# Moving batch 1's value chunks and key burst, and one unit pair of batch 2, in a block-sorted attention and SwiGLU kernel

## The chip, the cores and the metric

The kernel runs on one core of a Trainium2 chip. The core has a matrix engine (TensorE, PE in the profile, with its weight loads as PEld), three engines for the rest (VectorE or DVE, ScalarE or ACT, GpSimd or POOL), a queue engine for DMAs (SyncE or SP), and 16 DMA engines. The metric is the device time of one execution in microseconds (us). The kernel before takes 247.38 us, the median of three runs (247.33 to 247.43).

## The reference

Four batches, eight heads, 768 positions, head width 64. Keys and values are cut into eight blocks of 96 positions and mixed with a small matrix that five rounds of row and column normalisation make nearly doubly stochastic; then each block of queries attends to its mixed block. The result, 3072 tokens of width 512, goes through a SwiGLU feed-forward layer of inner width 1536.

```python
for _ in range(5):
    P = np.exp(P - np.max(P, axis=-1, keepdims=True))
    P = P / (np.sum(P, axis=-1, keepdims=True) + 1e-09)
    P = P / (np.sum(P, axis=-2, keepdims=True) + 1e-09)
k_sorted = np.einsum('bhij,bhjcd->bhicd', P, k_b)
v_sorted = np.einsum('bhij,bhjcd->bhicd', P, v_b)
attn = softmax(scale * q_b @ k_sb^T)            # block by block, 96 x 96
x = (attn @ v_sb), heads side by side           # 3072 x 512
g = x @ w_gate
out = (g * sigmoid(g) * (x @ w_val)) @ w_out    # 3072 x 512
```

## The kernel before

The tokens are worked on in eight half batches of 384 tokens. Half batch `n` (batch `n // 2`, half `n % 2`) has one **pass** of the feed-forward layer, `ffn(n)`: 12 gate bursts and 12 value bursts of four matmuls each (L410, L428), and, for the half batch before, three output tiles in three parts of four matmuls each (L445). The attention of a later half batch is worked in between these. A pass is written as `merge(ffn(n), side)` (L599): `ffn(n)` is a list of pieces with a cost (0.65 for a gate or value burst, 0.87 for an output part), `side` a list of pieces with a due time, and a side piece is issued after the first main piece with which the summed cost reaches its due time. `merge` sets the order on TensorE and GpSimd, which follow the program; in these passes the order on VectorE, ScalarE and SP is made by the scheduler when the kernel is built.

The side pieces:

- `kqs(b, ats)` (L588): three **key bursts** (with the queries) for a batch; each is two chunks of 32 matmuls (L269), the first into tile "b" and drained by VectorE, the second into tile "a" and drained by ScalarE.
- `vs(v_chunk, 16, ats)` (L592): batch 1's four **value chunks**, 16 matmuls each (L300), into "b", "a", "b", "a". In the string `"sssv"` s is ScalarE and v is VectorE: the engine that drains the chunk into `vt`.
- `units(b, us, ats, avs)` (L572): eight units per batch, in pairs. At `at` the **scores** of both units (`qk`, L332; the first into "b", the second into "a") with the first exp; at `at + 1.3` the second exp (L345, ScalarE); at `at + avs[0]` and `at + avs[1]` the attention times values (`av`, L359, into "b" and "a"), each followed by a reciprocal `r_sb` (L363) and a product `st` (L365) on VectorE and, from batch 1 on, by a transposing DMA on SP (L391) that writes a quarter of `xt`, the input of that half batch's pass.

"a" and "b" are one PSUM tile each: whoever writes one waits until its last reader is done. The gate, value and (in the second pass) output tiles rotate through three buffers called "gen", so each waits for the reader of the tile three before it. Outputs from the third pass on use a tile of their own, "x".

Behind a gate burst ScalarE computes `th` (tanh, L418) and VectorE `gs` (L420); behind a value burst VectorE computes `h` (L433). An output tile is copied by ScalarE (L450) and written by SP (L452). POOL issues `q_cast` (L394), which writes the queries of batches 2 and 3 to a scratch in DRAM, early in the second pass, and then waits at `hold` (L639) for the last quarter of batch 1's first `xt` before it loads the values of batches 2 and 3.

The passes of this case are the second, `ffn(1)` (L636), which holds batch 1's keys, values and first four units, the third, `ffn(2)` (L645), which reads the `xt` made there, and the fourth, `ffn(3)` (L647), with batch 2's first four units.

Of the kernel before, what the change touches and what calls it, by code (L numbers as in the profile page):

```python
# [17 lines left out]
def kernel(  # L18
# [226 lines left out]
    def drain(eng, dst, src):  # L245
        if eng == "v":
            nc.vector.tensor_copy(dst, src)  # L247
        else:
            nc.scalar.copy(dst, src)  # L249
# [13 lines left out]
    def kq_chunk(b, at, n, eng, tag):  # L263
        dst = kqt_tile(b)[:, 0:2 * GI * C].rearrange("p (n c) -> p n c", c=C)
        rm = rmix[b].rearrange("p a (g two) i -> p two (a g) i", two=2)
        tp = chunk_tile("tkq", n // 8, tag).rearrange("p (l n) -> p l n", n=2 * GI)
        for lc in range(n):
            for two in range(2):
                nc.tensor.matmul(tp[two * D:(two + 1) * D, lc, :],  # L269
                                 lhsT=kq_at(b, at + lc),  # L270
                                 rhs=rm[:, two], start=True, stop=True)
        drain(eng, dst[:, :, at:at + n], tp.transpose([0, 2, 1]))
# [31 lines left out]
    def v_pair_chunk(pair, at, n, eng, tag):  # L304
        dst = vt_tile(pair)[:, :, :, at:at + n]
        tp = chunk_tile("tv", n // 4, tag).rearrange("p (u l n) -> p u l n", u=2, n=H * NB)
        for ld in range(n):
            col = (at + ld) * C
            for u, rows in enumerate((lowr, highr)):
                nc.tensor.matmul(tp[:, u, ld, :], lhsT=vch[rows, col:col + 128],  # L310
                                 rhs=rmix["p"][rows, u].rearrange("p a b -> p (a b)"),
                                 start=True, stop=True)
        drain(eng, dst, tp[0:C].transpose([0, 1, 3, 2]))
# [4 lines left out]
    def scores(b, u, tag):  # L318
        half, g = divmod(u, H2)
        k_sb, k_at, q_sb, q_at = ((kqts[b], 0, kqts[b], GI * C) if b < 2 else  # L320
                                  (kqts["p"], (b - 2) * GI * C, kqts["q"], (b - 2) * GI * C))
        if tag == "gen":
            wide = None
            pss = [bank_tile("qk"), bank_tile("qk")]
        else:
            wide = pair_tile("qk", tag).rearrange("p (two n) -> p two n", two=2)
            pss = [wide[:, 0], wide[:, 1]]
        for i4 in range(4):
            at = (g * NB + half * 4 + i4) * C
            for two in range(2):  # L330
                lo = two * D
                nc.tensor.matmul(pss[two][:, i4 * C:(i4 + 1) * C],  # L332
                                 lhsT=k_sb[lo:lo + D, k_at + at:k_at + at + 128],
                                 rhs=q_sb[lo:lo + D, q_at + at:q_at + at + C],
                                 start=True, stop=True)
        return wide, pss

    def exps(b, u, wide, pss):
        n = ecount[0] % 8
        ecount[0] += 2  # L340
        if wide is None:
            for two in range(2):
                nc.scalar.activation(e_all[:, n + two, 0:4 * C], pss[two][0:C, 0:4 * C], AF.Exp, scale=scale)
        else:
            nc.scalar.activation(e_all[:, n:n + 2, 0:4 * C], wide[0:C, :, 0:4 * C], AF.Exp, scale=scale)  # L345
        es[(b, u)] = [e_all[:, n, :], e_all[:, n + 1, :]]

    def qk(b, u, tag="b"):
        exps(b, u, *scores(b, u, tag))

    def av(b, u, tag="a"):
        half, g = divmod(u, H2)
        vt = vts[b // 2][:, b % 2].rearrange("p (h i) e -> p h i e", h=H)
        av_ps = pair_tile("av_ps", tag).rearrange("p (two n) -> p two n", two=2)
        o = av_ps.rearrange("p two (i e) -> p two i e", i=4)
        for two in range(2):
            e = es[(b, u)][two]
            for i4 in range(4):
                nc.tensor.matmul(o[:, two, i4, 0:D + 1], lhsT=e[:, i4 * C:i4 * C + 128],  # L359
                                 rhs=vt[:, 2 * g + two, half * 4 + i4, 0:D + 1],  # L360
                                 start=True, stop=True)
        r_sb = ssp.tile([C, 2, 4, 1], FP32, name="r_sb", tag="r")
        nc.vector.reciprocal(r_sb, o[0:C, :, :, D:D + 1])  # L363
        st = ssp.tile([C, 4, 2, D], BF16, name="st", tag="st")
        nc.vector.tensor_tensor(st.rearrange("p i two d -> p two i d"), o[0:C, :, :, 0:D],  # L365
                                r_sb.to_broadcast([C, 2, 4, D]), op=ALU.mult)
        sts[(b, u)] = st
# [11 lines left out]
    def xtr(b, u):  # L379
        half, g = divmod(u, H2)  # L380
        if g == 0:
            xts[(b, half)] = xtp.tile([128, H2, TW], BF16, name=f"xt{b}_{half}", tag="xt")
        x_ps = xt_tile("x", 1)[:, 0]
        x_to(x_ps, b, u)
        return xts[(b, half)][:, g, :], x_ps.rearrange("p a b -> p (a b)")

    def x_dma(b, u):
        half, g = divmod(u, H2)
        if g == 0:
            xts[(b, half)] = xtp.tile([128, H2, TW], BF16, name=f"xt{b}_{half}", tag="xt")  # L390
        nc.sync.dma_start_transpose(out=xts[(b, half)][:, g, :].rearrange("p (i c) -> p i c", c=C),  # L391
                                    in_=sts.pop((b, u)).rearrange("p i two d -> p (i two d)"))
# [179 lines left out]
    def units(b, us, ats, avs=(1.9, 3.6), lag=3.1):  # L572
        us = list(us)
        todo = []
        for n, at in enumerate(ats):
            u, u2 = us[2 * n:2 * n + 2]
            held = []
            todo.append((at, lambda u=u, u2=u2, held=held: (qk(b, u, "b"), held.append(scores(b, u2, "a")))))
            todo.append((at + 1.3, lambda u2=u2, held=held: exps(b, u2, *held[0])))
            for w, tag, t in ((u, "b", avs[0]), (u2, "a", avs[1])):  # L580
                if b == 0:
                    todo.append((at + t, lambda w=w, tag=tag: av(b, w, tag)))
                    todo.append((at + t + lag, lambda w=w: drain("v", *xtr(b, w))))
                else:
                    todo.append((at + t, lambda w=w, tag=tag: (av(b, w, tag), x_dma(b, w))))
        return todo

    def kqs(b, ats):  # L588
        return [(at, lambda n=n: (kq_chunk(b, n * 32, 16, "v", "b"), kq_chunk(b, n * 32 + 16, 16, "s", "a")))
                for n, at in enumerate(ats)]  # L590

    def vs(f, size, ats):  # L592
        return [(at, lambda m=m: f(1, m * size, size, "sssv"[m], "ba"[m % 2])) for m, at in enumerate(ats)]

    def v_pairs(ats):
        return [(at, lambda m=m: (v_pair_chunk(1, m * 16, 8, "v", "b"), v_pair_chunk(1, m * 16 + 8, 8, "s", "a")))
                for m, at in ats]

    def merge(main, side):  # L599
        done, k = 0.0, 0  # L600
        side = sorted(side, key=lambda t: t[0])
        for c, f in main:
            f()
            done += c
            while k < len(side) and side[k][0] <= done:
                side[k][1]()
                k += 1
        while k < len(side):
            side[k][1]()
            k += 1  # L610

    def ffn(n):
        todo = []
        for m in range(NFC):
            if n > 0 or m > 1:
                todo.append((0.65, lambda m=m: gate(n, m)))
            if n > 0 or m > 0:
                todo.append((0.65, lambda m=m: value(n, m)))
            ends = (7, 9, 11) if n == 1 else (3, 7, 11)
            if n > 0 and m in ends:  # L620
                for part in range(3):
                    todo.append((0.87, lambda t3=ends.index(m), part=part: outp(n - 1, t3, part)))
        return todo
# [7 lines left out]
    def q0_rest():  # L631
        q0_chunk(1, 0, 16, "s", "b")
        q0_chunk(1, 16, 8, "v", "a")

    merge(ffn(0), [(0.0, q0_rest)] + units(0, range(4, 8), (2.0, 6.6)))
    merge(ffn(1), kqs(1, (0.6, 3.3, 7.8)) + vs(v_chunk, 16, (5.2, 6.5, 9.1, 10.4))  # L636
          + units(1, range(4), (11.0, 15.6), (1.3, 2.6)))
    hold = const.tile([1, 1], BF16)
    nc.gpsimd.tensor_copy(hold, xts[(1, 0)][0:1, H2 - 1, 0:1])  # L639
# [2 lines left out]
    for s in range(4):  # L642
# [1 line left out]
    nc.vector.memset(kqt_tile("p")[:, 2 * GI * C:], 0.0)  # L644
    merge(ffn(2), units(1, range(4, 8), (0.0, 5.5)) + kqs("p", (13.0, 14.7, 20.7)) + v_pairs([(0, 22.5)])  # L645
          + [(13.0, lambda: q_dma(2)), (16.4, lambda: q_dma(3))])
    merge(ffn(3), v_pairs([(1, 0.0), (2, 5.1), (3, 6.9)]) + units(2, range(4), (9.8, 14.0)))  # L647
    merge(ffn(4), units(2, range(4, 8), (0.0, 8.0)))
    merge(ffn(5), units(3, range(4), (0.0, 8.0)))
    merge(ffn(6), units(3, range(4, 8), (0.0, 8.0)))  # L650
# [36 lines left out]
```

## Time and profile before

| what | us |
| --- | --- |
| median of the runs | 247.38 |
| profiled execution | 247.53 |
| its span, first to last instruction | 245.7 |
| gate matmuls, L410 (376 in the records) | 76.6 |
| value matmuls, L428 (380) | 77.3 |
| output matmuls, L445 (276) | 64.4 |
| `th` on ScalarE, L418 (96) | 47.1 |
| `gs` on VectorE, L420 (96) | 52.9 |
| `h` on VectorE, L433 (96) | 53.3 |
| exps on ScalarE, L345 (30) | 22.6 |
| casts of `vt` on ScalarE, L249 (10) | 9.1 |
| casts of `vt` on VectorE, L247 (8) | 8.6 |
| third pass's first gate starts at | 75.72 |
| fifth pass's first gate starts at | 134.25 |

Of a few hundred matmuls some records are missing (384 gate matmuls are issued, 376 are recorded). In a timeline row the columns are start, length, engine, line, operation, output and input, count, and in brackets the idle time before it with what ended it. Matmuls are pipelined: the length of a burst of four is given as 0.81 us, while such bursts follow one another every 0.65 us. A burst's price is therefore read from starts, not from lengths.

### The profile page before, as it was taken

The numbers are of one execution on the slowest core, as the hardware profiler recorded it, in microseconds if no ns is written. First come the engines' busy times: TensorE is split into PE (matmuls) and PEld (weight loads), VectorE is DVE, ScalarE is ACT, GpSimd is POOL, SyncE is SP. The second block draws the span as 40 slices with busy tenths as digits, with TensorE's granted clock in tenths as the row PEclk, the third lists the DMA queues.
The fourth block names the chain that finished last, engine by engine and source line by source line (L and its number), as shares of the span: only waits on it lengthen the run. The fifth ranks groups of instructions, "written<-read, shape, count | busy, mean of one in ns | idle before, by whom it ended". The sixth has DMA issues, their size and how long they took to land.

```text
span 245.7 us, 6163 instructions
## 1 busy us (share of the span) xinstructions
PE 237.1 (97%) x2617; PEld 139.4 (57%) x2617; DVE 155.9 (63%) x327; ACT 111.2 (45%) x188; POOL 51.3 (21%) x45
## 2 busy tenths in 40 slices
PE   7799999998999999999999999999999999999994
PEld 5375666675555565555555655565555555555543
DVE  6786789877564685777655845664675576445700
ACT  3977653465444535365542543265235424332311
POOL 5992139990002059300000000000000000000000
PEclk9999999999999999999999999999999999999999
DMA  5989999999995999510121211112111211110122
GB/s 95 216 121 209 206 213 211 206 213 190 156 131 143 196 136 157 139 43 3 45 75 32 61 59 37 41 53 69 32 43 45 75 36 43 43 43 3 43 85 85
DMA packets 39642, 24.77 MB, mean 101 GB/s; under 512 B 29376, under 2 KB 34368, under 8 KB 39616
## 3 DMA queue, kind: packets, MB, share of 16 engines
q0 software_dynamic: 19632, 14.16, 38.7%
q1 hardware_dynamic: 19840, 10.17, 17.4%
q8 instruction: 20, 0.33, 0.6%
q10 hardware_dynamic: 144, 0.07, 0.1%
q14 instruction: 6, 0.05, 0.1%
HBM read 28.32 MB, written 7.86 MB: 147 GB/s over the span
## 4 chain that ended last, share of the span: by engine, by line
PE 86%; DVE 6%; issue 2%; DMA 2%; ACT 2%; DVEq 0%; POOLq 0%
PE v_ps L428 24%; PE g_ps L410 24%; PE o_ps L445 24%; PE tkq L269 3%; PE av_ps L359 3%; PE qk L332 3%; DMA v<-in_v_dram 2%; DVE st L365 1%; DVE vt L247 1%; DVE gs_sb L420 1%; PE o_ps L461 1%; PE idle_ps L477 1%; DVE h L433 1%; PE tq L279 1%; PE tv L300 1%
## 5 line engine op out<-in xcount | busy, mean ns | idle before, releaser
L420 DVE SCALAR_TENSOR_TENSOR gs_sb<-th_sb,g_ps 128x384 bf16<-128x384 bf16 x96 | 52.9, 551 | 49.5 <-ACT th_sb L418 46.4
L428 PE MATMUL v_ps<-xt,wv_sb 128*128 128x384 bf16 x380 | 77.3, 326 | 0.1
L410 PE MATMUL g_ps<-xt,wg_sb 128*128 128x384 bf16 x376 | 76.6, 325 | 0.2
L418 ACT ACTIVATE th_sb<-g_ps 128x384 bf16<-128x384 f32 x96 | 47.1, 491 | 56.2 <-PE g_ps L410 53.6
L445 PE MATMUL o_ps<-wo,h 128*128 128x512 bf16 x276 | 64.4, 379 | 0.0
L433 DVE SCALAR_TENSOR_TENSOR h<-v_ps,gs_sb 128x384 bf16<-128x384 f32 x96 | 53.3, 556 | 7.6 <-DVE gs_sb L420 0.5
L428 PEld LDWEIGHTS <-wv_sb 128*128 128x128 bf16 x380 | 35.5, 97 | 24.0 <-issue 0.7
L410 PEld LDWEIGHTS <-wg_sb 128*128 128x128 bf16 x376 | 34.8, 97 | 23.7 <-issue 0.6
L445 PEld LDWEIGHTS <-h 128*128 128x128 bf16 x276 | 26.0, 98 | 28.4
L450 ACT COPY o_sb<-o_ps 128x512 f32<-128x512 f32 x23 | 13.5, 586 | 46.0 <-PE o_ps L445 46.0
L148 POOL COPY vch<-v 64x1536 bf16<-64x1536 bf16 (+2 forms) x11 | 28.8, 2658 | 13.3 <-DMA v<-in_v_dram 13.3
L345 ACT ACTIVATE e_all<-qk 96x768 bf16<-96x768 f32 x30 | 22.6, 802 | 8.1 <-PE qk L332 8.1
L365 DVE TENSOR_TENSOR st<-av_ps,r_sb 96x512 bf16<-96x512 f32 x32 | 21.8, 680 | 0.3
L359 PEld LDWEIGHTS <-e_all 96*128 96x128 bf16 x256 | 11.9, 97 | 5.2 <-ACT e_all L345 0.9
L363 DVE RECIPROCAL r_sb<-av_ps 96x8 f32<-96x8 f32 x32 | 6.4, 199 | 11.5 <-PE av_ps L359 11.5
L359 PE MATMUL av_ps<-vt,e_all 96*128 96x65 bf16 x256 | 13.1, 193 | 0.0
L249 ACT CAST vt<-tv 96x1024 bf16<-96x1024 f32 (+1 forms) x10 | 9.1, 923 | 5.6 <-PE tv L310 3.6
L247 DVE CAST vt<-tv 96x1024 bf16<-96x1024 f32 (+1 forms) x8 | 8.6, 1082 | 2.2 <-PE tv L310 1.7
L477 PE MATMUL idle_ps<-warm_sb 128*128 128x512 bf16 x25 | 6.9, 382 | 0.0
L247 DVE COPY oq_v<-o_ps 128x128 f32<-128x128 f32 x1 | 0.3, 293 | 9.3 <-PE o_ps L461 9.3
L395 POOL DMA_DIRECT2D q_scr<-in_q_dram x2 | 5.6, 3178 | 0.0
L146 ACT COPY vch<-v 64x768 bf16<-64x768 bf16 (+1 forms) x4 | 5.5, 1388 | 0.3 <-DMA v<-in_v_dram 0.3
(83 smaller groups left out, 130.2 us busy)
## 6 DMA issues: line engine op xcount, KB each, us to landing
out_dram<-o_sb SPq DMA_DIRECT2D x23, 256.0 KB, 2.0
v<-in_v_dram POOLq DMA_DIRECT2D x4, 384.0 KB, 12.7
wg_sb<-in_moe_w_gate_dram POOLq DMA_DIRECT2D x3, 512.0 KB, 11.4
wv_sb<-in_moe_w_val_dram POOLq DMA_DIRECT2D x3, 512.0 KB, 13.2
wo<-in_moe_w_out_dram POOLq DMA_DIRECT2D x3, 512.0 KB, 16.0
kqp<-in_k_dram POOLq DMA_DIRECT2D x2, 768.0 KB, 10.1
q_scr<-in_q_dram POOLq DMA_DIRECT2D x2, 768.0 KB, 17.8
v<-in_v_dram POOLq DMA_DIRECT2D x2, 768.0 KB, 9.8
```

Source lines behind the costliest of these rows:

```text
L148: eng.tensor_copy(dst, src.transpose([0, 2, 1]))
L247: nc.vector.tensor_copy(dst, src)
L345: nc.scalar.activation(e_all[:, n:n + 2, 0:4 * C], wide[0:C, :, 0:4 * C], AF.Exp, scale=scale)
L359: nc.tensor.matmul(o[:, two, i4, 0:D + 1], lhsT=e[:, i4 * C:i4 * C + 128], rhs=vt[:, 2 * g + two, half * 4 + i4, 0:D + 1], start=True, sto ...
L365: nc.vector.tensor_tensor(st.rearrange("p i two d -> p two i d"), o[0:C, :, :, 0:D], r_sb.to_broadcast([C, 2, 4, D]), op=ALU.mult)
L410: nc.tensor.matmul(g_ps, lhsT=wg_sb[:, kc, ts(m, 128)], rhs=xt[:, kc, :], start=(kc == 0), stop=(kc == NKC - 1))
L418: nc.scalar.activation(th_sb, g_ps, AF.Tanh, scale=0.5)
L420: nc.vector.scalar_tensor_tensor(gs_sb, th_sb, 1.0, g_ps, op0=ALU.add, op1=ALU.mult)
L428: nc.tensor.matmul(v_ps, lhsT=wv_sb[:, kc, ts(m, 128)], rhs=xt[:, kc, :], start=(kc == 0), stop=(kc == NKC - 1))
L433: nc.vector.scalar_tensor_tensor(h_tiles[n][:, m, :], v_ps, 0.5, gs_tiles.pop(m), op0=ALU.mult, op1=ALU.mult)
L445: nc.tensor.matmul(o_ps, lhsT=h_w[:, m, ts(t3, 128)], rhs=wo_sb[part][:, m % 4, :], start=(m == 0), stop=(m == NFC - 1))
L450: nc.scalar.copy(o_sb, o_ps)
```

## The change

Three edits, all in due times and one string:

- In the second pass the last three value chunks are due at 5.8, 8.4 and 9.1 instead of 6.5, 9.1 and 10.4, and the third key burst at 7.1 instead of 7.8. The second value chunk now follows gate burst 4 instead of value burst 4; the third key burst follows gate 5 instead of value 5; the third value chunk follows gate 6 instead of value 6; the fourth follows value 6 instead of value 7.
- The fourth value chunk is drained by ScalarE instead of VectorE.
- In the fourth pass batch 2's second unit pair is due at 14.9 instead of 14.0. Its scores follow the third part of the second output tile instead of its second part, its first `av` follows value burst 8 instead of gate burst 8, and its second `av` follows gate burst 10 instead of value burst 9.

```diff
     def vs(f, size, ats):
-        return [(at, lambda m=m: f(1, m * size, size, "sssv"[m], "ba"[m % 2])) for m, at in enumerate(ats)]
+        return [(at, lambda m=m: f(1, m * size, size, "s", "ba"[m % 2])) for m, at in enumerate(ats)]
...
-    merge(ffn(1), kqs(1, (0.6, 3.3, 7.8)) + vs(v_chunk, 16, (5.2, 6.5, 9.1, 10.4))
+    merge(ffn(1), kqs(1, (0.6, 3.3, 7.1)) + vs(v_chunk, 16, (5.2, 5.8, 8.4, 9.1))
           + units(1, range(4), (11.0, 15.6), (1.3, 2.6)))
...
-    merge(ffn(3), v_pairs([(1, 0.0), (2, 5.1), (3, 6.9)]) + units(2, range(4), (9.8, 14.0)))
+    merge(ffn(3), v_pairs([(1, 0.0), (2, 5.1), (3, 6.9)]) + units(2, range(4), (9.8, 14.9)))
```

With it the scheduler's order moves in three places. On VectorE the drain of the third key burst stands ahead of `h` of value burst 5 instead of behind it, and the cast of the fourth value chunk is gone. On ScalarE the casts of the third and fourth value chunks stand together ahead of `th` of gate burst 7. In the fourth pass the copy of the second output tile stands ahead of the second pair's two exps instead of behind them, and VectorE's `r_sb`, `st`, `gs` and `h` of gate and value bursts 8 to 10 take another order: `gs`, `r_sb`, `h`, `st` of the first unit, then the second unit's `r_sb` and `st` behind `gs` and around `h` of burst 10. SP's and GpSimd's orders are the same.

## The prediction

> **What bounds the kernel now.** First the page. The profiled execution took 247.53 us with a span of 245.7 us at full granted clock; the median of the runs shown is 247.38 us.
>
> ```profile
> span 245.7 us, 6163 instructions
> PE 237.1 (97%) x2617; PEld 139.4 (57%) x2617; DVE 155.9 (63%) x327; ACT 111.2 (45%) x188; POOL 51.3 (21%) x45
> PE 86%; DVE 6%; issue 2%; DMA 2%; ACT 2%; DVEq 0%; POOLq 0%
> ```
>
> TensorE works 97% of the span and is 86% of the chain that ended last. The change keeps every matmul, so it can only win or lose TensorE's idle time in the two passes it touches. One pass is one `merge(ffn(n), ...)`. From start of one pass to the next I read 32.6 us for the second (43.1 to 75.72) and 28.5 us for the fourth (105.78 to 134.25).
>
> Second, the waits of TensorE: the longest single one is a score matmul waiting for a value chunk drained by VectorE. The timeline shows where (start, length, engine, line, operation).
>
> ```profile
> PE qk L332 <- DVE vt L247: 1.0, 1, 1.0
> ...
> 59.02 0.63 PE L300 MATMUL tv<-rmix,vch 128*128 128x64 bf16 x16
> 59.49 1.03 PE L445 MATMUL o_ps<-wo,h 128*128 128x512 bf16 x4
> 60.45 0.34 PE L332 MATMUL qk<-kqt 64*128 64x96 bf16 x8
> 60.49 1.21 DVE L247 CAST vt<-tv 96x1024 bf16<-96x1024 f32 x1
> 61.75 0.35 PE L332 MATMUL qk<-kqt 64*128 64x96 bf16 x8 [0.96 <-DVE vt L247]
> 62.03 1.90 PE L445 MATMUL o_ps<-wo,h 128*128 128x512 bf16 x8
> ```
>
> The fourth value chunk (59.02) fills tile "a"; its VectorE drain starts at 60.49, behind `gs` and `h` of the FFN, and ends at 61.70; the second half of the scores needs "a". Bursts follow each other by start-to-start pitch: gate or value 0.65 us, output part 0.87, `av` 0.245, a pair of scores 0.45 (118.64 to 119.09 below), key burst 1.13, value chunk 0.47, and 0.09 more before scores or a key burst (117.90 to 118.64 is 0.74). So the output part after these scores was due at 60.45 + 0.45 = 60.90 and came at 62.03: 1.13 us lost. Another 0.19 is lost where the third value chunk starts at 57.26 instead of 56.42 + 0.65 = 57.07, waiting for VectorE's drain of the third key burst.
>
> Third, the fourth pass around batch 2's two unit pairs.
>
> ```profile
> 118.64 0.51 PE L332 MATMUL qk<-kqtq,kqtp 64*128 64x96 bf16 x16
> 119.03 1.50 ACT L345 ACTIVATE e_all<-qk 96x768 bf16<-96x768 f32 x2 [0.47 <-PE qk L332]
> 120.43 0.49 ACT L418 ACTIVATE th_sb<-g_ps 128x384 bf16<-128x384 f32 x1
> 120.64 0.81 PE L410 MATMUL g_ps<-xt,wg_sb 128*128 128x384 bf16 x4
> 120.95 0.55 DVE L420 SCALAR_TENSOR_TENSOR gs_sb<-th_sb,g_ps 128x384 bf16<-128x384 bf16 x1 [1.14 <-ACT th_sb L418]
> 121.55 0.81 PE L428 MATMUL v_ps<-xt,wv_sb 128*128 128x384 bf16 x4
> ...
> 124.27 0.77 PE L332 MATMUL qk<-kqtq,kqtp 64*128 64x96 bf16 x16
> 124.97 1.04 PE L445 MATMUL o_ps<-wo,h 128*128 128x512 bf16 x4
> ```
>
> The second pair's scores (124.27 to 124.97) take 0.70 instead of 0.45: 0.25 lost waiting for "a", which VectorE's `st` frees at 124.64. The first pair teaches more: two exps hold ScalarE from 119.03, so the `tanh` of the gate issued just after the scores starts at 120.43, its `gs` ends at 121.50, and the value matmul that reuses that gate's bank (three banks rotate) starts at 121.55 instead of 120.64 + 0.65 = 121.29.
>
> Fourth, the transposing DMAs that bring batch 1's first half to the third pass, on SP's queue.
>
> ```profile
> q0 software_dynamic: 2467, 0.31, 246.2%
> ...
> 70.53 2.16 SPq L391 DMA_TRANSPOSE xt<-st  x1
> 72.74 0.58 SPq L452 DMA_DIRECT2D out_dram<-o_sb  x1
> 73.37 1.22 SPq L391 DMA_TRANSPOSE xt<-st  x1
> ...
> 75.74 0.18 POOL L639 COPY hold<-xt 1x1 bf16<-1x1 bf16 x1 [20.82 <-DMA xt<-st]
> ```
>
> The first line is the DMA view of 64 to 66 us: only the software queue (the `q_cast` writes) moves, though SP issued an output at 64.58 and a transpose at 65.17; these land after the writes, which end near 71. The fourth transpose, at 73.37, has landed when POOL's `hold` starts (75.74); the pass's first gate (75.72) needs it for its fourth matmul at 75.72 + 0.49 = 76.21. Slack about 0.5 us.
>
> **Second pass, worked out.** PE issues the same bursts in the order gate 4, value chunk 2, value 4, gate 5, key burst 3, value 5, gate 6, chunk 3, value 6, chunk 4, gate 7, value 7, output, scores. From gate 4 at 51.47 the pitches give chunk 2 at 52.12, key burst 3 at 53.98, chunk 3 at 56.41, chunk 4 at 57.56, output part 59.34, scores 60.30. Each needs its tile free:
> - Chunk 2 ("a"): ScalarE's drain of key burst 2, 49.80 + 1.01 = 50.81. Free.
> - Key burst 3: "b" from chunk 1's drain, 51.67 + 1.01 = 52.68; its second half at 54.54 needs "a", drained by ScalarE from about 53.2 to 54.2. Free, by 0.3.
> - Chunk 3 ("b"): VectorE takes the key drain ahead of `h` of value 5, which the change moves behind it; from 55.18 it takes 1.21, to 56.39. A stall of 0.03.
> - Chunk 4 ("a"): ScalarE's key drain from 55.21 to 56.22. Free.
> - Scores: ScalarE drains chunk 3 from 57.11 and chunk 4 from 58.22 to 59.23. Free by 1.07, which is this edit's cover; without it every late microsecond of ScalarE is TensorE's.
>
> What ScalarE pays: one more 1.01 drain in place of VectorE's 1.21, and the `tanh` of gate 7 at 59.23 instead of 58.88. Its `gs` ends at 60.31; gate 8 needs that bank at 62.73. Cost nothing. So 0.19 + 1.13 - 0.03 = **1.29 us gained**. The bounds are nothing (the gain returned at the next pass, below) and 1.32.
>
> **Fourth pass, worked out.** The scores move behind the third output part, the first `av` behind value 8, the second behind gate 10. On ScalarE the output copy now stands ahead of the exps. From output part 2 at 123.31: part 3 at 124.18, scores 125.13 ("a" free since 124.64: the 0.25 stall goes), gate 8 125.58, value 8 126.23, `av` 126.89, gate 9 127.13. ScalarE: the copy starts 1.08 after its burst does (124.97 to 126.05 now), so 125.26, takes 0.59, then two exps by 0.71 each to the next issue, so `tanh` of gate 8 at 127.27. `gs` follows at 127.80 and ends at 128.35 (before, the `tanh` of gate 8 stood at 126.69). Value 9 needs gate 8's bank at 127.78 and starts at 128.40: a stall of 0.62. VectorE is now behind, with `r`, `h`, `st`, `gs` of gate 9 ending near 130.0, so value 10 waits 0.12 more. From there the pitches put the last three output parts at 132.03 against 131.66 before: **0.37 us lost**. Bounds: the naive reading, nothing but the vanished stall, gains 0.25; twice the exp queue's stall would lose 1.0. I take 0.37, because the same arithmetic on the first pair gives the 121.55 of the row.
>
> What is late next: the last `st` of batch 2's first half ends at 132.28 instead of 130.52, behind `h` of value 10. Its transpose lands 2.3 later (73.37 to 75.7 above), 134.6; the fifth pass's first gate wants it at 134.62 + 0.49 = 135.11. Hidden, by 0.5. SP's and POOL's orders stay as they are; no DMA is added.
>
> **The sum.** 247.53 - 1.29 + 0.37 = 246.61 for the profiled execution, which stands 0.15 above the median: 247.38 - 0.92 = **246.46 us**.
>
> **The rule that speaks against it.** In the third pass everything should come 1.29 earlier, but the `q_cast` writes end near 71 whatever TensorE does, and while they run the row of 64 to 66 us shows SP's queue moving nothing. The Trainium skill (DMA: Bandwidth & Descriptors, Queues, rings and completion order) says that each DMA engine takes turns between its queues, packet by packet; by it the transposes would shift with TensorE and the whole 1.29 stands. The row does not show turns. By the row, the first two transposes still land near 71.5 and 71.8, far ahead of 74.43, where the pass would start.
>
> The third and fourth are what counts. Shifted, the third is issued at 69.24 and, if it again takes 2.16, ends at 71.40; output 0.58 and gaps of 0.05 put the fourth at 72.08, landed at 74.4, needed at 74.43 + 0.49 = 74.92. I cost it at nothing, with 0.5 us of cover. POOL's value loads behind `hold` move with it; their last copies end at 100.1 (88.86 + 11.27 in POOL's row), and the first chunk that reads them starts at 104.33.
>
> **Rivals.**
> - *The fourth pass costs nothing* (12%). For it: TensorE only loses the 0.25 stall if ScalarE runs the gate's `tanh` early. Against: the built order puts copy, exps, `tanh` in this row. 247.38 - 1.29 - 0.25 = 245.84.
> - *The writes hold the transposes* (10%), the slower side. If the third transpose, started inside the writes, only gets its 2.16 once they end (71.05), it ends at 73.21, the fourth starts at 73.89 and lands at 76.2, so the first gate loses 76.2 - 74.92 = 1.28. Then 247.38 - 1.29 + 1.28 + 0.37 = 247.74. It decides for slower from a landing after 75.84. For it: 2.16 against 1.18 to 1.29 for nearly all others. Against: the second transpose, issued at 66.56 inside the writes, took 1.19.
> - *The fourth pass costs more* (12%): the last transpose's 0.5 of cover goes because its issue takes 1 us longer, like the 2.16 above; 0.47 more, 246.93.
>
> **How the numbers follow.** The forecast has 66%, with an own range from no loss in the fourth pass (247.38 - 1.29 = 246.1) to its bound (247.38 - 1.29 + 1.0 = 247.1). Range 246.0 to 247.2, which leaves out most of the first two rivals. A change under 0.2% (0.49 us) can't be told from none here. Faster: 0.61 of the forecast's 0.66, the first rival's 0.12, 0.05 of the third, 0.78; slower: 0.06 from the second; the rest, 0.16, same.
>
> **What would show it.** In the profile after, right if the wait of `qk` for `vt` is gone from TensorE's waits and output part 1 starts near 60.75 instead of 62.03; the third pass starts near 74.4 with no hole in its first gate; and a hole near 0.6 stands before the value matmul of gate 9 in the fourth pass. Wrong if the first gate of the third pass waits for a transpose, if `tanh` of gate 8 isn't behind the exps, or if TensorE's holes elsewhere change.

## The result and the profile after

The changed kernel takes 246.38 us (median of 5 runs, 246.32 to 246.54), the kernel before 247.43 us in the same comparison: a ratio of 0.9954 with a 95% interval of 0.9942 to 0.9965. It is 1.05 us faster; 0.92 was forecast. Ratios are taken over the fast runs alone, so they need not equal the ratio of the medians (0.9958 here); one run below, at 249.16 us, was a slow one.

The page of the kernel after: span, engines, chain of the work that ended last.

```profile
span 244.7 us, 6163 instructions
PE 237.1 (97%) x2617; PEld 139.5 (57%) x2617; DVE 154.6 (63%) x326; ACT 112.0 (46%) x189; POOL 51.2 (21%) x45
PE 88%; DVE 5%; ACT 2%; DMA 2%; issue 2%; POOLq 0%
```

TensorE is busy for the same 237.1 us in a span 1.0 us shorter: only idle time went. One drain moved from VectorE's count to ScalarE's.

TensorE's new wait, and the timeline of the second pass (start, length, engine, line, operation; in brackets idle time and what ended it). Of each timeline, here and below, only the rows that bear on the text are shown.

```profile
PE v_ps L428 <- DVE gs_sb L420: 0.3, 1, 0.3
```

```profile
57.07 2.12 ACT L249 CAST vt<-tv 96x1024 bf16<-96x1024 f32 x2
57.52 0.63 PE L300 MATMUL tv<-rmix,vch 128*128 128x64 bf16 x16
59.10 0.49 ACT L418 ACTIVATE th_sb<-g_ps 128x384 bf16<-128x384 f32 x1
59.29 1.03 PE L445 MATMUL o_ps<-wo,h 128*128 128x512 bf16 x4
60.25 0.51 PE L332 MATMUL qk<-kqt 64*128 64x96 bf16 x16
60.69 1.90 PE L445 MATMUL o_ps<-wo,h 128*128 128x512 bf16 x8
```

The wait of `qk` for `vt` has left the list; a wait of a value burst for `gs` has come in. ScalarE's two casts end at 59.19, a microsecond before the scores, which run in one piece; the output part behind them starts at 60.69 where it was 62.03.

The fourth pass:

```profile
123.86 0.51 PE L332 MATMUL qk<-kqtq,kqtp 64*128 64x96 bf16 x16
123.96 0.59 ACT L450 COPY o_sb<-o_ps 128x512 f32<-128x512 f32 x1 [3.25 <-PE o_ps L445]
124.44 1.51 ACT L345 ACTIVATE e_all<-qk 96x768 bf16<-96x768 f32 x2
125.84 0.49 ACT L418 ACTIVATE th_sb<-g_ps 128x384 bf16<-128x384 f32 x1
125.86 0.81 PE L410 MATMUL g_ps<-xt,wg_sb 128*128 128x384 bf16 x4
126.37 0.55 DVE L420 SCALAR_TENSOR_TENSOR gs_sb<-th_sb,g_ps 128x384 bf16<-128x384 bf16 x1 [3.00 <-ACT th_sb L418]
126.97 0.81 PE L428 MATMUL v_ps<-xt,wv_sb 128*128 128x384 bf16 x4 [0.30 <-DVE gs_sb L420]
```

This is the chain that was forecast: copy, two exps, `tanh` of gate 8, `gs`, and only then value burst 9. Gate 9 starts at 125.86, so that burst was due at 126.51; the hole is 0.46 us by starts (the bracket counts from the modelled end of the gate and says 0.30).

Last, SP's queue, the third pass's first gate and `hold` behind the last transpose.

```profile
69.20 1.18 SPq L391 DMA_TRANSPOSE xt<-st  x1
70.42 2.05 SPq L452 DMA_DIRECT2D out_dram<-o_sb  x1
72.52 1.21 SPq L391 DMA_TRANSPOSE xt<-st  x1
...
74.38 0.88 PE L410 MATMUL g_ps<-xt,wg_sb 128*128 128x384 bf16 x4
74.95 0.18 POOL L639 COPY hold<-xt 1x1 bf16<-1x1 bf16 x1 [19.89 <-DMA xt<-st]
75.19 0.51 PE L332 MATMUL qk<-kqt 64*128 64x96 bf16 x16
```

The pass starts 1.34 earlier than before, but `hold` only 0.79 earlier (74.95 for 75.74). The gate's four matmuls take 0.88 instead of 0.81, and the scores follow 0.81 after the gate's start instead of 0.75: about 0.06 us lost on the last transpose. The rows before:

```profile
75.72 0.81 PE L410 MATMUL g_ps<-xt,wg_sb 128*128 128x384 bf16 x4
76.47 0.51 PE L332 MATMUL qk<-kqt 64*128 64x96 bf16 x16
```

From starts alone, in us: second pass from its gate 3 (bursts are counted from 0; it starts at 49.69 before and 49.67 after), third and fourth pass from first gate to next first gate.

| kernel | gate 3 to third pass | third pass | fourth pass |
| --- | --- | --- | --- |
| before | 26.03 | 30.06 | 28.47 |
| after | 24.71 | 30.12 | 28.67 |

So -1.32, +0.06 and +0.20, in sum -1.06. The forecast had -1.29, 0 and +0.37, so the sum came out as near as it did in part by luck: the fourth pass's loss, taken 0.17 too large, covers the 0.06 that wasn't forecast.

### The profile page after: what moved, and what is told of

It is laid out like the page before. It is cut to its first block, busy times and chain, and to the rows that moved or that the text cites. A ratio compares the mean times of both kernels' runs of the same rounds, so it can differ in the third digit from the quotient of the medians.

```text
span 244.7 us, 6163 instructions
## 1 busy us (share of the span) xinstructions
PE 237.1 (97%) x2617; PEld 139.5 (57%) x2617; DVE 154.6 (63%) x326; ACT 112.0 (46%) x189; POOL 51.2 (21%) x45
## 4 chain that ended last, share of the span: by engine, by line
PE 88%; DVE 5%; ACT 2%; DMA 2%; issue 2%; POOLq 0%
PE v_ps L428 25%; PE o_ps L445 25%; PE g_ps L410 24%; PE tkq L269 3%; PE av_ps L359 3%; PE qk L332 3%; DMA v<-in_v_dram 2%; PE o_ps L461 1%; PE idle_ps L477 1%; DVE gs_sb L420 1%; PE tv L300 1%; DVE st L365 1%; DVE vt L247 1%; PE tq L279 1%; PE tv L310 1%
## 5 line engine op out<-in xcount | busy, mean ns | idle before, releaser
L249 ACT CAST vt<-tv 96x1024 bf16<-96x1024 f32 (+1 forms) x11 | 10.1, 931 | 4.7 <-PE tv L310 3.6
L247 DVE CAST vt<-tv 96x1024 bf16<-96x1024 f32 (+1 forms) x7 | 7.4, 1064 | 2.2 <-PE tv L310 1.7
```

## The experiments

The kernel before took 247.51 us in the comparison of the first four runs and 247.48 in that of the last three; what a single pass gained or lost is read from its stretch, as in the table.

**Undo the fourth pass's edit.**

```diff
-... units(2, range(4), (9.8, 14.9)))
+... units(2, range(4), (9.8, 14.0)))
```

> The changed kernel with batch 2's second unit pair back at 14.0; the second pass as changed. Theory (the second pass gains about 1.3 us and the moved pair costs TensorE 0.2, since its exps stand ahead of a gate's tanh): 0.2 us under the changed kernel, about 246.15 us, 1.25 under before; fifth pass's first gate 1.28 earlier than before. Rival (the moved pair is a gain that the fourth pass gives back elsewhere, or costs nothing): 246.4 or more.

Measured: 246.13 us against 247.51 before, ratio 0.9943 (0.9929 to 0.9956), 0.25 under the changed kernel. Its three stretches are 24.71, 30.09 and 28.49: the second pass's gain whole, the fourth pass as before. The moved pair costs about 0.2 us.

**The fourth pass's edit alone**, on the kernel before.

```diff
-... units(2, range(4), (9.8, 14.0)))
+... units(2, range(4), (9.8, 14.9)))
```

> The kernel before with only batch 2's second unit pair moved to 14.9. Theory: 0.2 us slower than before, about 247.6 us, with a hole of 0.46 us ahead of the value burst that follows gate burst 9 and no 0.25 us hole in the scores. Rival (the pair's move pays, by the 0.25 us of the vanished stall): 247.15 us.

Measured: 247.56 us against 247.51, ratio 1.0004 (0.9995 to 1.0012). The time excludes the rival's 247.15, but can't tell a loss of 0.2 from none. The stretches can: 26.03, 30.05 and 28.67, the fourth 0.20 longer, with value burst 9 at 128.11 behind a gate at 126.99 (0.47 late) and the scores in 0.45 instead of 0.70. So the 0.25 stall vanishes here too, and the hole that comes in its place is larger.

**The due times alone**, the fourth chunk drained by VectorE as before; fourth pass as before.

```diff
-... f(1, m * size, size, "s", "ba"[m % 2])) ...
+... f(1, m * size, size, "sssv"[m], "ba"[m % 2])) ...
-... units(2, range(4), (9.8, 14.9)))
+... units(2, range(4), (9.8, 14.0)))
```

> The second pass with the new due times but the fourth value chunk drained by VectorE as before; fourth pass as before. Theory A (the drain was late because the chunk was issued last; two bursts earlier VectorE has it done by 59.5 us, 0.8 before the second scores want tile a): the whole 1.25 us gain, 246.15 us. Theory B (VectorE's queue is the bound, so the drain by ScalarE makes the gain): a hole before the second scores stays, 246.7 us or more.

Measured: 246.08 us, ratio 0.9943 (0.9931 to 0.9956); stretches 24.71, 30.06, 28.49. This is theory A. The timeline shows VectorE's drain and the scores:

```profile
58.08 1.21 DVE L247 CAST vt<-tv 96x1024 bf16<-96x1024 f32 x1
...
60.07 0.52 PE L332 MATMUL qk<-kqt 64*128 64x96 bf16 x16
```

VectorE is done at 59.29, 0.8 us before the scores start. With the chunk issued two bursts sooner, the engine that drains it makes no difference.

**The drain by ScalarE alone**, old due times; fourth pass as before.

```diff
-... kqs(1, (0.6, 3.3, 7.1)) + vs(v_chunk, 16, (5.2, 5.8, 8.4, 9.1))
+... kqs(1, (0.6, 3.3, 7.8)) + vs(v_chunk, 16, (5.2, 6.5, 9.1, 10.4))
-... units(2, range(4), (9.8, 14.9)))
+... units(2, range(4), (9.8, 14.0)))
```

> The second pass with the old due times but the fourth value chunk drained by ScalarE; fourth pass as before. Theory (ScalarE is free at 59.7 us and ends the drain at 60.75, when the second scores are due at 60.77, so the 1.1 us hole goes; the 0.2 us hole at the third value chunk stays): about 246.35 us. Rival (ScalarE's queue only moves the hole, since its exps follow): 246.9 us or more.

Measured: 246.43 us, ratio 0.9957 (0.9945 to 0.997); stretches 25.03, 30.05, 28.49. So 1.00 of the 1.32 us comes with this edit alone. The timeline shows what is left:

```profile
57.13 0.63 PE L300 MATMUL tv<-rmix,vch 128*128 128x64 bf16 x16
...
59.56 1.01 ACT L249 CAST vt<-tv 96x1024 bf16<-96x1024 f32 x1 [0.37 <-PE tv L300]
60.32 0.65 PE L332 MATMUL qk<-kqt 64*128 64x96 bf16 x16
60.90 1.90 PE L445 MATMUL o_ps<-wo,h 128*128 128x512 bf16 x8
```

The third value chunk still starts 0.19 late (57.13 for 56.29 + 0.65, value burst 6 being at 56.29), and the scores take 0.58 instead of 0.45, since ScalarE's cast ends at 60.57, when their second half is due.

**Scores behind a gate in the fourth pass**, second pair.

```diff
-... units(2, range(4), (9.8, 14.9)))
+... units(2, range(4), (9.8, 15.7)))
```

> The changed kernel with batch 2's second unit pair due at 15.7: its scores follow gate burst 8 instead of the third output part, so ScalarE does that gate's tanh ahead of the two exps. Theory (the hole of 0.46 us ahead of value burst 9 is that tanh standing behind copy and exps): the hole and the 0.10 us behind it are gone, fifth pass's first gate near 132.6 instead of 133.17, about 245.8 us. Rival (exps cost TensorE their time wherever they stand, VectorE being behind): the hole moves to a later burst, 246.2 us or more.

Measured: 245.81 us, ratio 0.9931 (0.9917 to 0.9946); fourth pass 28.09 instead of 28.67. The timeline:

```profile
123.68 0.81 PE L410 MATMUL g_ps<-xt,wg_sb 128*128 128x384 bf16 x4
124.43 0.51 PE L332 MATMUL qk<-kqtq,kqtp 64*128 64x96 bf16 x16
124.53 0.49 ACT L418 ACTIVATE th_sb<-g_ps 128x384 bf16<-128x384 f32 x1
124.92 1.50 ACT L345 ACTIVATE e_all<-qk 96x768 bf16<-96x768 f32 x2
```

The pair's `av` move with the scores, the first behind value burst 9. `tanh` of gate 8 now stands ahead of the exps, and the hole ahead of value burst 9 is gone: it starts at 126.19, 0.66 behind gate 9. None takes its place: the pass is 0.58 shorter than in the changed kernel.

**Both pairs behind a gate.**

```diff
-... units(2, range(4), (9.8, 14.9)))
+... units(2, range(4), (10.5, 15.7)))
```

> As the kernel before this in the list, and batch 2's first pair due at 10.5 too, so that its scores follow gate burst 6 instead of value burst 5. Theory: the first pair's hole (0.26 us ahead of value burst 7) goes as well, 0.85 us under the changed kernel, about 245.55 us, faster than both kernels; the last transpose of the half batch lands some 0.25 us before the fifth pass wants it. Rival (that transpose comes late, since the pair's products are later): a hole in the fifth pass's first gate, 245.8 us or more.

Measured: 245.60 us (median of 8 runs), ratio 0.9936 (0.9914 to 0.9959). Six of the eight lie between 245.48 and 245.63, under all four of the kernel above (245.75 to 245.83), but two, 247.95 and 249.16, lie far above, and the interval overlaps that of the kernel above. The fourth pass tells the two apart, 27.86 for 28.09. The first pair:

```profile
118.11 0.49 ACT L418 ACTIVATE th_sb<-g_ps 128x384 bf16<-128x384 f32 x1 [0.85 <-PE g_ps L410]
118.45 0.82 PE L428 MATMUL v_ps<-xt,wv_sb 128*128 128x384 bf16 x4
118.50 1.50 ACT L345 ACTIVATE e_all<-qk 96x768 bf16<-96x768 f32 x2
119.11 0.81 PE L410 MATMUL g_ps<-xt,wg_sb 128*128 128x384 bf16 x4
119.77 0.81 PE L428 MATMUL v_ps<-xt,wv_sb 128*128 128x384 bf16 x4
```

Gate 7 and value 7 are 0.66 apart; before they were 0.91 apart. The fifth pass's first gate shows no hole (132.33, its scores 0.74 later), so the last transpose still came in time. By medians this is the fastest kernel here: 0.78 us under the changed one, 1.88 under the one before.

**Half of the small writes.** The cast of batch 3's queries to DRAM goes behind the value loads.

```diff
     q_cast(2)
-    q_cast(3)
...
     load_v(3, 0, 4)
+    q_cast(3)
```

> The changed kernel with the query cast of batch 3 issued behind the value loads instead of ahead of them, so that half of the small writes are gone when the second pass's transposes are issued. Theory (these writes delay SP's queue): the first transpose, issued near 63.8, lands by 67 instead of 71.3, the fourth by 73.4 instead of 74.9, and the 0.07 us hole in the third pass's first gate is gone; time within 0.2 us of the changed kernel unless the moved writes delay the third pass's transposes, which would be a hole in the fourth pass's first gate. Rival (the delay is not from the writes): landings as in the changed kernel.

Measured: 248.37 us (median of 9 runs, 248.02 to 250.66), ratio 1.0057 (1.0034 to 1.008), slower than before. The timeline:

```profile
70.41 0.58 SPq L452 DMA_DIRECT2D out_dram<-o_sb  x1
71.03 1.20 SPq L391 DMA_TRANSPOSE xt<-st  x1
73.43 0.18 POOL L638 COPY hold<-xt 1x1 bf16<-1x1 bf16 x1 [20.43 <-DMA xt<-st]
...
104.56 1.22 SPq L391 DMA_TRANSPOSE xt<-st  x1
106.93 0.32 PE L410 MATMUL g_ps<-xt,wg_sb 128*128 128x384 bf16 x1 [1.86 <-DMA xt<-st]
```

Both halves of the expectation held. The first transpose, issued at 63.81, landed 3.0 us later instead of 7.5, the fourth by 73.43, and the third pass's first gate has no hole (scores 0.75 behind it). The fourth comes 1.5 us sooner than in the changed kernel because the output ahead of it takes 0.58 us on SP's queue instead of 2.05; from its own issue to `hold` it takes 2.4 us in both (71.03 to 73.43, 72.52 to 74.95). But SP's second load of the transposed queries needs these writes; it started at 100.28 instead of 92.67 in the changed kernel and held the last transpose of the third pass until 104.56, and the fourth pass's first gate waited 1.86 us for it.

## Why the prediction was right, and where it was off

- *The second pass gains 1.29.* Measured 1.32. The list of free times held throughout; the 0.03 us stall allowed at chunk 3 didn't come, since VectorE began the key drain at 55.06 instead of 55.18. The prediction took the edit as one. The runs show that its two parts each remove the large hole: the due times alone give all 1.32, the drain by ScalarE alone 1.00. In the changed kernel ScalarE's drain adds nothing that the times hadn't brought.
- *ScalarE pays nothing for the drain.* Held: `tanh` of gate 7 at 59.10, nothing waits for it.
- *The fourth pass loses 0.37.* The mechanism was right, the term was too large: it measured 0.18 to 0.20, shown three ways (after against before, undone, alone). The part that was mis-sized is the stall of 0.62 at value burst 9, which measured 0.46. The arithmetic let the first exp start 0.59 after the output copy's start; it started 0.48 after (123.96 to 124.44), as the two overlap. Rows of the kernel before had this overlap: the exps of 124.65 end at 126.15, and the copy behind them starts at 126.05.
- *The rule and the row on SP's queue.* Here a step failed, though it was worth only 0.06 us: the last transpose was costed at nothing with 0.5 us of cover, and SP's queue was taken to be held until the writes end, near 71 us. The first gate of the third pass did wait for a transpose, which the prediction named as a sign of being wrong. The forecast had the third transpose take 2.16 again and the output behind it 0.58, so that the fourth is issued at 72.08. The third took 1.18, the output 2.05, and the fourth was issued at 72.52 and had landed at 74.95 instead of 74.4. The queue wasn't held until the writes end either, as the DMA views show.

Kernel before, 68 to 69 us:

```profile
q0 software_dynamic: 762, 0.10, 151.4%
q1 hardware_dynamic: 75, 0.15, 43.1%
```

Kernel after, 67 to 68 us:

```profile
q0 software_dynamic: 449, 0.06, 89.2%
q1 hardware_dynamic: 116, 0.24, 69.6%
```

SP's queue (q1) first moves some 4 us after its output is issued (issued at 64.58 before and 63.24 after, first packet at 68.5 and 67.1), not when the writes (q0) end; in the microsecond ahead of these rows there is only q0, 1238 and 1237 packets. From then on both move. That agrees with the turn-taking of the Trainium skill (DMA: Bandwidth & Descriptors, Queues, rings and completion order), which the prediction had set aside for the row of 64 to 66 us; the 4 us between the output's issue and the first packet stay unexplained. With half of the writes they shrink to 0.9 (63.22 to 64.1). The writes also last longer than the forecast had them: from 71 to 72 us q0 has 154 packets after and none before. The last transpose moved by 0.79 us while the pass moved by 1.34, so the cover of 0.5 was used up and 0.06 was lost. The run with half of the writes shows that they delay the first transpose (3.0 us to landing for 7.5). For the fourth, the one that counts, it shows only that with fewer writes the output ahead of it isn't slow; why it is slow beside all of them stays open. In the other kernels with this second pass and this third pass the loss is 0.03 (fourth pass undone) or none (the two with scores behind a gate). The slower rival looked in the right place, but its mechanism did not come: the third transpose, started inside the writes, took 1.18, and the landing, which it needed after 75.84, came by 74.95.
- *The other two rivals.* A fourth pass that costs nothing is refuted by the two runs that move only this edit. A late last transpose in the fifth pass (scores 0.74 behind its first gate, as where none is late) came neither in the changed kernel nor in the two that make the fourth pass shorter.

## What to carry to other kernels

When a buffer that two stages share comes free too late, try first to issue the work that fills it earlier: here that alone brought all 1.32 us, and giving its drain to another engine brought 1.00. Where a long instruction (here two exps, 1.5 us) enters an engine's queue, put it behind the short one on which the next buffer depends: in the fourth pass scores issued after a gate burst opened no hole, and scores issued before one opened holes of 0.26 and 0.46 us. And when a pass is pulled forward, look up each transfer that it waits for: it may move by less than the pass does.

## What wasn't expected of the hardware

- An output that SP issued while a GpSimd queue was writing pieces of 128 bytes moved its first packet 3.5 to 4 us after its issue in all eight kernels with all of these writes, and 0.9 us after it with half of them; there the first transpose landed after 3.0 us in place of 7.5.
- One SP instruction that starts between 70.2 and 71.3 us took 1.9 to 2.3 us in eight of the nine kernels: before, the third transpose (2.16); after, the output behind it (2.05); with the due times alone, the fourth transpose (2.28). In all eight the DMA records have a packet of the instruction queue that ends while this instruction runs (before 72.28, after 72.09), 0.4 us ahead of its end in six of them and 1.1 us in the two where it is the fourth transpose. In the ninth, with half the writes, that packet ran from 68.9 to 69.8, and the transpose of 69.18 to 70.36 took its usual 1.18. That is a coincidence in nine traces, not a tested cause.
